# A fused retention and SwiGLU kernel: rows through GpSimd's queue, paired attention units, one PSUM rotation, half groups

## The chip, the cores and the metric

One core of one Trainium2 chip. The metric is device time in microseconds (us) of one execution, smaller is better. Most executions of one kernel agree within 1%; where one is over 1.5% above the fastest of its kernel, it counts as slow and stays out of the ratios. Ratios are the mean time of one kernel's fast runs over the mean of the other's fast runs of the same rounds on the same chip, so they are not quite the ratio of the medians quoted beside them.

Engines: PE (matmul), PEld (its weight loads), DVE (vector), ACT (scalar), POOL (GpSimd), SP (only issues transfers here). "PE waits" is idle time of PE just before an instruction, put down to what released it.

## The reference, cut to what matters

```python
# q, k, v: (B=4, H=8, S=768, D=64) float32
for t in range(S):                                   # retention, decay gamma[h]
    state = gamma * state + k[:, :, t] (x) v[:, :, t]
    y[:, :, t] = scale * q[:, :, t] @ state
x = y as (3072 tokens, 512)
xn = x / sqrt(mean(x*x) + 1e-6) * rms_g
out = (silu(xn @ w_gate) * (xn @ w_val)) @ w_out     # d_ff = 1536
```

Both kernels cut the sequence into six chunks c0 to c5 of 128 positions and turn the retention of a chunk into matmuls: scores (k against q, masked), y = masked scores against v plus q against the running state, and kv, which is added to the state. A **unit** is one chunk of one batch entry with all eight heads. The FFN of a chunk works on 512 tokens (four units): 12 gate-value blocks of 4 + 4 matmuls of 512 columns, then 4 down projections of 12. A **slot** is one block or one down projection; the attention of the next chunk is put between the slots of the present one. Names in the code and the profile: qb and kb are rows of q and k in bf16, qT and kT their transposes; a_ps are scores and am masked scores; x is y scaled, rstd its normalising factor (made on POOL from a sum of squares), xn the normalised rows and xnT their transpose; sg and hT are a block's results, o_sb that of a down projection.

## The kernel before

```python
def load(c, b, after=None):                # rows in float32, by SP
    for name, src in (("q_f", q), ("k_f", k), ("v_f", v)):
        x = loads.tile([128, H, D], F32, name=name)
        nc.sync.dma_start(out=x, in_=...)
# ...
def cast(c, b):                            # POOL casts, SP transposes
    nc.gpsimd.tensor_copy(qb, q_f...)
    nc.gpsimd.tensor_copy(kb, k_f...)
    nc.gpsimd.tensor_tensor(out=vp, in0=v_f, in1=vdec..., op=ALU.mult)
    if c > 1:
        for n in "qk":
            nc.sync.dma_start_transpose(out=t, in_=d[n + "b"])
# ...
def piece_y(c, b):                         # y, state, kv; x; squares; rstd on POOL
# ...
def piece_n(c, b):
    nc.vector.scalar_tensor_tensor(out=xn, in0=x, scalar=d["rstd"], in1=g_bc, ...)
    nc.sync.dma_start_transpose(out=cur[c, "xnT"][...], in_=xn)      # c > 1
# ...
PLAN = dict(cast=(0, 1, 2, 3), t=..., a=(4, 6, 8, 10), y=(6, 8, 10, 12),
            n=(8, 10, 12, 13), x=(8, 10, 12, 14))     # slot of each piece, by unit
# ...
def gv(n):
    g_ps = fps.tile([128, GT], F32, name="g_ps", tag="ff")   # one PSUM bank each
    v_ps = fps.tile([128, GT], F32, name="v_ps", tag="ff")
# ...
def down(b, n0=0, n1=NFF):                 # own bank for each
    o_t[b] = fps.tile([128, DM], F32, name="o_ps", tag="ff")
    # ... matmuls
    nc.scalar.copy(o_sb, o_ps)
    nc.sync.dma_start(out=out_v[c, b], in_=o_sb)
# ... in the loop over slots:
            if c == 0 and i == 16:         # chunk 2's rows, after the w_out weights
                nc.sync.dma_start(out=g_bc, ...)
                for b in range(B):
                    load(2, b, after=landed["wo", 2])
            if 0 < c < NCH - 2 and i in (5, 7, 9, 11):
                load(c + 2, (i - 5) // 2)
```

In chunks 2 to 5 the q and k transposes of the next chunk are thus requested in slots 0 to 3, the xn transposes in slots 8 to 13, both from SP. Chunks 0 and 1 are transposed on PE.

## Time and profile before

250.92 us (250.68 to 251.89); the profiled execution has a span of 248.7 us.

| stage (first gate matmul to the next) | us | PE busy |
|---|---|---|
| head, to the first gate matmul | 24.4 | 14.1 |
| c0 | 41.1 | 38.8 |
| c1 | 39.1 | 35.7 |
| c2, c3 | 36.8 each | 35.7 |
| c4 | 35.5 | 34.8 |
| c5 and tail | 35.1 | 31.1 |

PE is nearly full after the head. SP issues 63 row loads in the background, and PE waits for one transpose only, for 2.3 us in c1. The lines that show this stand in the prediction below.

### The profile page before, as it was taken

The numbers are of one execution on the slowest core, as the hardware profiler recorded it, in microseconds if no ns is written. First come the engines' busy times: TensorE is split into PE (matmuls) and PEld (weight loads), VectorE is DVE, ScalarE is ACT, GpSimd is POOL, SyncE is SP. The second block draws the span as 40 slices with busy tenths as digits, with TensorE's granted clock in tenths as the row PEclk, the third lists the DMA queues.
The fourth block names the chain that finished last, engine by engine and source line by source line (L and its number), as shares of the span: only waits on it lengthen the run. The fifth ranks groups of instructions, "written<-read, shape, count | busy, mean of one in ns | idle before, by whom it ended". The sixth has DMA issues, their size and how long they took to land.

```text
span 248.7 us, 4121 instructions
## 1 busy us (share of the span) xinstructions
PE 225.9 (91%) x1495; PEld 114.4 (46%) x1521; DVE 128.1 (51%) x215; ACT 87.4 (35%) x170; POOL 95.2 (38%) x177
## 2 busy tenths in 40 slices
PE   1776999979996989999989999989999999999993
PEld 0553445545433545445544445544444444444443
DVE  4796337676234895036894046894047781134300
ACT  6365334531431242232342322433232422332221
POOL 8978144953850236910246910246900211000000
PEclk9997999999999999999999999999999999999999
DMA  9999999898997699955999356999453114200022
GB/s 140 174 195 203 196 219 221 151 199 167 218 290 109 144 222 189 229 127 87 213 209 175 127 131 98 199 207 209 122 115 66 21 21 129 86 0 0 0 87 86
DMA packets 108213, 35.94 MB, mean 145 GB/s; under 512 B 99040, under 2 KB 104928, under 8 KB 108192
## 3 DMA queue, kind: packets, MB, share of 16 engines
q1 hardware_dynamic: 95232, 29.24, 60.8%
q0 software_dynamic: 12288, 6.29, 19.0%
q8 instruction: 12, 0.20, 0.3%
q10 hardware_dynamic: 672, 0.13, 0.3%
q14 instruction: 9, 0.07, 0.1%
HBM read 28.58 MB, written 6.29 MB: 140 GB/s over the span
## 4 chain that ended last, share of the span: by engine, by line
PE 77%; DVE 10%; DMA 5%; issue 3%; ACT 3%; POOL 0%; SPq 0%; DVEq 0%; ACTq 0%
PE o_ps L361 24%; PE v_ps L338 21%; PE g_ps L335 21%; DVE am L219 4%; PE a_ps L215 3%; PE y_ps L232 2%; DMA v_f<-in_v_dram 2%; DVE x L247 2%; DMA k_f<-in_k_dram 2%; PE kv_ps L244 1%; PE y_ps L237 1%; DMA kT<-kb 1%; DVE xn L283 1%; PE o_ps L351 1%; PE qk_ps L199 1%
## 5 line engine op out<-in xcount | busy, mean ns | idle before, releaser
L341 DVE TENSOR_TENSOR hT<-sg,v_ps 128x512 bf16<-128x512 bf16 x72 | 49.4, 687 | 89.6 <-PE v_ps L338 83.2
L338 PE MATMUL v_ps<-xnT,wv_b 128*128 128x512 bf16 x282 | 73.4, 379 | 0.5
L335 PE MATMUL g_ps<-xnT,wg_b 128*128 128x512 bf16 x276 | 72.9, 380 | 0.4
L340 ACT ACTIVATE sg<-g_ps 128x512 bf16<-128x512 f32 x72 | 42.8, 594 | 63.7 <-PE g_ps L335 62.2
L361 PE MATMUL o_ps<-wo_b,hT 128*128 128x512 bf16 x269 | 60.8, 379 | 1.2 <-DMA wo_b<-in_moe_w_out_dram 0.8
L338 PEld LDWEIGHTS <-wv_b 128*128 128x128 bf16 x288 | 28.2, 98 | 34.0
L335 PEld LDWEIGHTS <-wg_b 128*128 128x128 bf16 x288 | 26.6, 98 | 31.5 <-issue 0.9
L361 PEld LDWEIGHTS <-hT 128*128 128x128 bf16 x276 | 26.6, 98 | 30.9 <-issue 0.8
L272 POOL TENSOR_SCALAR ms<-ssq 128x1 f32<-128x1 f32 x24 | 4.5, 189 | 92.4 <-ACT xsq L251 92.3
L251 ACT ACTIVATE xsq<-x 128x512 f32<-128x512 f32 x24 | 15.1, 630 | 48.7 <-DVE x L247 48.6
L219 DVE TENSOR_TENSOR am<-a_ps,causal 128x512 bf16<-128x512 f32 x48 | 30.8, 682 | 2.4 <-PE a_ps L215 2.4
L366 ACT COPY o_sb<-o_ps 128x512 f32<-128x512 f32 x23 | 13.5, 585 | 36.8 <-PE o_ps L361 30.7
L180 POOL TENSOR_TENSOR vp<-v_f,vdec 128x512 bf16<-128x512 f32 x20 | 20.7, 1037 | 3.4 <-DMA v_f<-in_v_dram 3.4
L268 POOL CAST st_b<-st_f 64x256 bf16<-64x256 f32 x40 | 17.3, 432 | 1.3
L247 DVE TENSOR_TENSOR x<-y_ps,ydec 128x512 f32<-128x512 f32 x24 | 16.4, 685 | 1.4 <-PE y_ps L237 0.8
L232 PE MATMUL y_ps<-vp,am 128*128 128x64 bf16 x192 | 12.0, 200 | 5.4 <-DVE am L219 5.1
L178 POOL CAST qb<-q_f 128x512 bf16<-128x512 f32 x20 | 12.1, 606 | 8.7 <-DMA q_f<-in_q_dram 7.9
L283 DVE SCALAR_TENSOR_TENSOR xn<-x,rstd,g_bc 128x512 bf16<-128x512 f32 x16 | 12.5, 784 | 5.5 <-POOL rstd L275 5.5
L232 PEld LDWEIGHTS <-am 128*128 128x128 bf16 x192 | 9.2, 101 | 13.1 <-DVE am L219 9.7
L275 POOL TENSOR_TENSOR rstd<-ms,mhalf 128x1 f32<-128x1 f32 x24 | 13.2, 552 | 2.0
L179 POOL CAST kb<-k_f 128x512 bf16<-128x512 f32 x20 | 12.2, 609 | 2.6 <-DMA k_f<-in_k_dram 1.7
L259 DVE TENSOR_TENSOR st_f<-st_f,kv_ps 128x512 f32<-128x512 f32 x16 | 10.8, 676 | 0.0
(60 smaller groups left out, 125.5 us busy)
## 6 DMA issues: line engine op xcount, KB each, us to landing
out_dram<-o_sb SPq DMA_DIRECT2D x23, 256.0 KB, 2.2
q_f<-in_q_dram SPq DMA_DIRECT2D x21, 256.0 KB, 4.8
k_f<-in_k_dram SPq DMA_DIRECT2D x21, 256.0 KB, 5.0
v_f<-in_v_dram SPq DMA_DIRECT2D x21, 256.0 KB, 5.1
wg_b<-in_moe_w_gate_dram POOLq DMA_DIRECT2D x4, 384.0 KB, 9.6
wv_b<-in_moe_w_val_dram POOLq DMA_DIRECT2D x4, 384.0 KB, 10.7
wo_b<-in_moe_w_out_dram POOLq DMA_DIRECT2D x3, 512.0 KB, 8.3
v_f<-in_v_dram POOLq DMA_DIRECT2D x3, 256.0 KB, 6.2
```

The source lines that it names most:

```text
L180: nc.gpsimd.tensor_tensor(out=vp, in0=v_f, in1=vdec[:, c, :, None].to_broadcast([128, H, D]), op=ALU.mult)
L219: nc.vector.tensor_tensor(out=am[:, i], in0=a_ps[i], in1=causal[:, None, :].to_broadcast([128, NHP, 128]), op=ALU.mult)
L232: nc.tensor.matmul(y_ps[:, h, :], d["am"][:, i, hp, :], d["vp"][:, h, :], start=first, stop=last, skip_group_check=True)
L247: nc.vector.tensor_tensor(out=x, in0=y_ps, in1=ydec[:, c, :, None].to_broadcast([128, H, D]), op=ALU.mult)
L251: nc.scalar.activation(xsq, x.rearrange("p h d -> p (h d)"), AF.Square, accum_out=ssq)
L268: nc.gpsimd.tensor_copy(st_b[b][r, :, i * 64:i * 64 + 64], st_f[b][r, :, i * 64:i * 64 + 64])
L283: nc.vector.scalar_tensor_tensor(out=xn, in0=x, scalar=d["rstd"], in1=g_bc, op0=ALU.mult, op1=ALU.mult)
L335: nc.tensor.matmul(g_ps, wg_b[:, s, sl], xnT[:, s, :], start=s == 0, stop=s == KS - 1)
L338: nc.tensor.matmul(v_ps, wv_b[:, s, sl], xnT[:, s, :], start=s == 0, stop=s == KS - 1)
L340: nc.scalar.activation(sg, g_ps, AF.Silu)
L341: nc.vector.tensor_tensor(out=hT[:, n, :], in0=sg, in1=v_ps, op=ALU.mult)
L361: nc.tensor.matmul(o_ps, hT[:, n, b * C:(b + 1) * C], wo_b[:, n, :], start=n == 0, stop=n == NFF - 1)
```

## The change

Its intent: fewer casts (a transfer by GpSimd's queue can cast float32 to bf16), less work on DVE in chunk 0 (the decay goes into the mask), fewer changes of PE's row tiling (two units per row-tiled phase), shorter holes (FFN blocks begin when three of the four units are ready; chunk 1 in two half groups of 256 columns) and one rotation of four two-bank PSUM tiles for everything. The diff, cut to its core:

```diff
-    aps = tile_pool(name="aps", bufs=4, PSUM);  fps = tile_pool(name="fps", bufs=4, PSUM)
+    psum = tile_pool(name="psum", bufs=1, PSUM)
+    def banks(name, dtype=F32):               # tiles p0..p3 in turn, two banks each
+        i = turn[0] % 4
+        turn[0] += 1
+        return psum.tile([128, 2, 512 ...], dtype, name=name, tag=f"p{i}")
-    i = nc.sync.dma_start(out=x, in_=src[b]...)            # float32, then casts on POOL
+    def load(c, b, names="qkv"):
+        nc.gpsimd.dma_start(out=x (bf16 for q and k), in_=srcs[n][c, b])
+    def t_dma(c, b):
+        for n in "qk":
+            nc.sync.dma_start_transpose(out=t, in_=u[n])
+    nc.scalar.activation(mask0, marg, AF.Exp, scale=1.0, bias=lnscale)   # decay in c0's mask
+    def pair_pe(c, bs, nxt=()):               # scores of next units, state and y of two
+    def gv(c, n0, n1, t0, t1):
+        ps = banks("gv_ps")                   # bank 0 gate, bank 1 value
+        nc.scalar.activation(sg, ps[:, 0, :m], AF.Silu)
+        nc.vector.tensor_tensor(out=HT..., in0=sg, in1=ps[:, 1, :m], op=ALU.mult)
+    def down(c, b, n0=0, n1=NFF):
+            if b % 2 == 0:
+                O[c] = banks("o_ps")          # two down projections share a tile
+        ps = O[c, b][:, b % 2, :]
@@ head @@
+    gv(0, 0, 1, 0, 384)
+    rstd(0, [3])
+    load_w(4, 6)
+    norm(0, 3)
+    x_pe(0, 3)
@@ chunk 1: steps 0 to 15 are 6 double blocks + 2 down, twice @@
+        0: [..., L(load, 2, 0)],   1: [..., L(load, 2, 1)],
+        2: [..., L(load, 2, 2), L(t_dma, 2, 0), L(t_dma, 2, 1)],   3: [..., L(load, 2, 3)],
+        6: [..., L(t_dma, 2, 2), L(t_dma, 2, 3), L(load, 3, 0), L(begin, 2)],
@@ chunks 2 to 5, d = c + 1 @@
+                3: [L(pair_pe, d, (0, 1), ((d, 2), (d, 3))), ...],
+                6: [L(norm, d, 0), L(norm, d, 1), L(x_dma, d, 0), L(x_dma, d, 1)]
+                   + [L(state_cast, 0), L(state_cast, 1), L(t_dma, d + 1, 0), L(t_dma, d + 1, 1)] * state,
+                9: [L(pair_pe, d, (2, 3), ((d + 1, 0), (d + 1, 1)) if state else ())] ...
+                11: [L(norm, d, 2), L(norm, d, 3), L(x_dma, d, 2), L(x_dma, d, 3)] ...
+                12: [L(t_dma, d + 1, 2), L(t_dma, d + 1, 3)] * state,
```

## The prediction

> **What bounds the kernel now.** I read the share of each engine first, then a table of busy time by stage, then the timeline of the matmul engine, then the waits. The page:
>
> ```profile
> PE 225.9 (91%) x1495; PEld 114.4 (46%) x1521; DVE 128.1 (51%) x215; ACT 87.4 (35%) x170; POOL 95.2 (38%) x177
> PE   1776999979996989999989999989999999999993
> PEclk9997999999999999999999999999999999999999
> ```
>
> PE is full except in the first four slices, so the end is set by PE's list of work plus the holes in it. The stages begin where the first gate matmul of each FFN chunk begins in the timeline (24.38, 65.4, 104.5, 141.3, 178.2, 213.8); the table cut there (start:end and length, then busy us of each engine with instruction counts, clock, DMA share, GB/s):
>
> ```profile
> 0.00:24.38 24.38, 14.11 (x133) 9.44 (x135) 17.09 (x42) 14.04 (x30) 20.38 (x39) 0.93 1.38 178
> 24.38:65.59 41.21, 38.96 (x285) 20.30 (x289) 22.54 (x36) 15.22 (x27) 21.74 (x40) 1.00 1.10 194
> 65.59:104.70 39.11, 35.75 (x238) 17.62 (x240) 20.58 (x32) 12.05 (x24) 18.35 (x33) 1.00 1.04 201
> 104.70:141.29 36.59, 35.46 (x235) 17.54 (x239) 20.49 (x32) 12.05 (x24) 14.61 (x29) 1.00 0.88 161
> ```
>
> The first 24.4 us are a chain through DMA, DVE, ACT and PE; after it every chunk is PE work. How much of a chunk is needed comes from start-to-start times in PE's timeline:
>
> ```profile
> 119.90 1.03 PE L335 MATMUL g_ps<-xnT,wg_b 128*128 128x512 bf16 x4
> 120.76 0.81 PE L338 MATMUL v_ps<-xnT,wv_b 128*128 128x512 bf16 x3
> 121.62 0.40 PE L232 MATMUL y_ps<-vp,am 128*128 128x64 bf16 x8
> 121.86 0.39 PE L237 MATMUL y_ps<-st_b,qT 128*128 128x128 bf16 x4
> 122.08 0.39 PE L244 MATMUL kv_ps<-vp,kb 128*128 128x128 bf16 x4
> 122.40 0.40 PE L215 MATMUL a_ps<-qT,kT 64*128 64x128 bf16 x8
> 122.73 1.04 PE L335 MATMUL g_ps<-xnT,wg_b 128*128 128x512 bf16 x4
> ```
>
> Four N=512 matmuls take 0.86 us, 0.216 each. An FFN chunk has 96 + 48 of them, 31.1 us; six chunks 186.7. One unit of attention takes 0.24 (y) + 0.22 (state) + 0.32 (kv, and the change to 64 rows) + 0.33 (scores, and the change back) = 1.11 us. Four N=128 matmuls need 0.22, so each change of row tiling costs about 0.1 us. Transposes on PE, for chunks 0 and 1 alone, add 0.45 + 0.22 per unit. Needed and measured: c0 31.1 + 4 x 1.78 = 38.2 of 41.0; c1 31.1 + 4.4 = 35.6 of 39.1; c2 and c3 35.6 of 36.8 and 36.9; c4 (no kv) 34.7 of 35.6; c5 31.1 of 31.1. So **9.7 us are holes**. The waits name the largest ones:
>
> ```profile
> PE y_ps L232 <- DVE am L219: 5.1, 14, 0.5
> PE a_ps L215 <- DMA kT<-kb: 2.3, 1, 2.3
> ```
>
> The last unit of each chunk is scheduled with one FFN slot between scores and their use, while DVE is behind; and in c1 a transpose by DMA queued on SP behind late input. The last matmul begins at 244.6 and 3.8 us of eviction, store and end follow.
>
> **What the Trainium skill says.** "TensorE: Matmul & The Clock Gate", Back-to-back issue gap, gives N/2.4 + 2.5 ns for a warm matmul, 215.8 ns at N=512 and 109.2 at N=256; the trace agrees with the first (0.216 us). "TensorEngine Tiling (Array Packing)", Key Properties: "Mode switching requires drain"; the trace agrees, with the 0.1 us above. "PSUM — Partial Sum Buffer", PSUM bank collisions, wants two engines kept off one bank and quadrant; the trace shows the order kept: the half copies of qk_ps, one bank, ran ACT from 6.79 and DVE only from 7.41. "DMA: Bandwidth & Descriptors", SWDGE vs HWDGE, says that a cast in a DMA must come from GpSimd, which builds the descriptors; the trace shows GpSimd held 0.9 us by each such load.
>
> **The change, part by part.**
>
> *Rows via GpSimd.* It removes 40 casts (12.1 + 12.2 us) from POOL and adds 63 issues of about 0.9 us = 57 us; the state cast becomes one instruction instead of two (17.3 us becomes an estimated 12). POOL then has about 125 us over 245, no bound on average. On the wire it helps: in the slice 6.0 to 6.5 us, cast rows alone in flight,
>
> ```profile
> q0 software_dynamic: 616, 0.08, 245.3%
> ```
>
> 616 packets per half microsecond, so 0.85 us for a 1024-piece q or k; v takes 1.2 us by the same reading. Before, SP's rows moved 0.11 MB per half microsecond, 1.17 us each. A unit falls from 3.5 to 2.9 us. In steady chunks this was hidden anyway, but the late transposes of c1 (2.3 us) should go: issue comes earlier and nothing waits for a cast.
>
> *Head.* POOL's issue rate decides it:
>
> ```profile
> 4.87 0.90 POOL L78 DMA_DIRECT2D qb<-in_q_dram  x1
> 10.09 0.83 POOL L149 DMA_DIRECT2D wg_b<-in_moe_w_gate_dram  x1
> 12.36 0.57 POOL L275 TENSOR_TENSOR rstd<-ms,mhalf 128x1 f32<-128x1 f32 x1
> ```
>
> Issue starts at 0.9 us; twelve loads, the first 1.1, the others 0.88 pitch, and two iotas (0.35) end at 12.05. I take q at 4.7 and k at 5.7. Transposes, copies and scores: 7.2; mask 1024 wide (two of 0.6 pitch) 8.45. Unit 1's scores end at 9.6, y0 at 9.95, its squares at 10.8. But rstd of unit 0 must wait for POOL: 12.05 to 12.85. Then two weight issues (1.6), rstd 1 (0.8), two more (1.6), vp of unit 2 on POOL (1.05): 17.9. y, squares 19.1, rstd 19.95; DVE still has mask 3 until 21.25, norm 22.0, transposes and copies 22.85; y3 and kv of units 0 and 1: 23.4, warm-up, first gate matmul near **23.8** instead of 24.4. Against that, unit 3's normalisation and two kv stand between the first FFN pieces (0.3 + 0.45 us and narrow matmuls): block n=2 begins at 28.5, where before it began at 27.8. So "three batches on" gains almost nothing: what the missing y-scaling (0.69 us of DVE per unit) frees is lost to POOL's queue. I call the head +0.7 us.
>
> *Decay in the mask.* Four DVE x instructions (2.7 us) go, one exp over 1024 elements and one 1024-wide multiply come, during the wait for q. It is inside the head above.
>
> *Pairs.* Per pair: scores 16 x 0.027 = 0.43, state 0.4 in the same row tiling, y 0.48, kv 0.44, changes 0.2: 1.95 against 2.22; 10 pairs give about 2.5 us. The state matmuls have half the columns, but the y matmuls show 0.03 us each at 64 columns, so no more than that is to be had.
>
> *Order and PSUM.* Scores of the next pair are made one pair early (six FFN slots ahead), so y never waits for its mask. One rotation of four two-bank tiles: a gate-value block leaves its banks about 1 us after its last matmul, a mask pair 2.6 us after, and a tile comes round after four. Following a steady chunk slot by slot (1.73 us each; DVE 0.7 hT, 2.4 masks, 1.2 y, 1.2 kv, 1.4 norm) I find waits of 0.3 us in all. Holes of 1.2 + 1.3 + 0.9 in c2 to c4 become about 1.0.
>
> *Half groups.* Chunk 1 uses 192 N=256 matmuls: 192 x 0.1092 = 21.0 against 20.75 us, +0.2. It lets units 2 and 3 of chunk 1 move beside its first half.
>
> **Sum.** Block n=2 at 28.5; ten blocks 17.3, hole 0.5: 46.3. Down of c0 10.4, half of chunk 1's attention 3.3, hole 1.0: 61.0. Chunk 1: 21.0 + 10.4 + other half 3.2 + chunk 2's attention and chunk 3's first scores 4.4 + holes 1.5: 101.5. c2, c3: 31.1 + 3.5 + 0.4 = 35.0 each. c4 33.5, c5 31.1, end 3.85: span 240.0. The time before was 2.2 above its span (250.92, 248.7), so **242.2 us**; I put 242.0. The gain of 8.9 is mostly holes (9.7 to about 4.5), 2.5 from pairs, the rest from work that is shifted, less 0.7 in the head.
>
> **Rivals.** (a) *POOL's queue becomes the wait*: rows, weights, vp, rstd and state casts stand in one order, and an issue that waits for a buffer holds rstd behind it. For: the head chain above is POOL's, and ms waited 92 us for squares with the queue empty behind it; now loads stand there. Against: 12 issues x 0.9 + 4 vp x 1.04 + 3 + 2.5 = 20 us of 35 per chunk. If two stages lose 2.5 us each: 247. (b) *The single PSUM rotation stalls gate-value blocks* when DVE is behind, in c1 above all, where DVE has an estimated 21 us in eight slots of about 21 us: +3 to +5, 246. (c) *Weights come late*, since rows and rstd stand before them: before, 0.39 MB pieces landed 2 us apart, and I find each 2 to 5 us ahead of use; if not, +2, 244. (d) *The head does gain* because first rows land sooner or DVE is the true bound, which is now lighter: FFN at 21, total 239. (e) *All holes vanish*: 237.
>
> **Range and chances.** d and e go below, a to c above, each perhaps one in four, rarely together: 236.5 to 247.0. Faster by over 2% needs under 245.9: that fails if a or b is full size, so 0.80; same 0.17; slower 0.03, since over 10 us of new waits would be needed beside the gains.
>
> **What would show it.** Right: first gate matmul at 23 to 25 us, n=2 near 28.5; steady chunks 34.5 to 35.5 with PE waits for am gone; two changes of row tiling per pair of 0.1 us; c1 39 to 41 us; POOL near 125 us busy. Wrong: gate matmuls waiting for hT, masks or o_sb (b), rstd or vp late on POOL with xn behind it (a), waits for wg_b or wv_b (c).

## The result, and the profile after

The changed kernel takes **308.82 us** (305.24 to 310.06, 4 runs) against 251.4 (250.68 to 253.13, 4 runs) for the kernel before on the same chip: ratio 1.2183 (95% interval 1.2086 to 1.228). It is slower by 22%, where 4% faster was predicted. The profiled execution is the slowest of the four (1.6% above the fastest, so it counts as slow); its losses are tens of us and come back in the profiles of fast runs below (c1 takes 66.8 us in `own` and 67.0 in `norm`, c2 46.8 in `norm`).

The page of the changed kernel, shares and PE's slices:

```profile
PE 243.4 (79%) x1718; PEld 129.1 (42%) x1718; DVE 126.9 (41%) x203; ACT 85.4 (28%) x171; POOL 124.9 (41%) x163
PE   4656899979947399179991989990989999899994
PEclk9999799999989579859997899998799999999999
```

PE is idle for 65 us, in deep holes (3, 1, 1, 0) that lie in c1 to c3, and its granted clock falls in or after each. By stage (start:end and length; busy us of PE, PEld, DVE, ACT, POOL with counts; granted clock; DMA share; GB/s):

```profile
26.91:71.25 44.34, 38.80 (x253) 19.41 (x252) 17.43 (x28) 14.07 (x28) 26.06 (x35) 0.96 1.06 143
71.25:141.27 70.02, 48.06 (x449) 32.68 (x448) 31.53 (x42) 14.67 (x32) 42.45 (x50) 0.83 1.25 126
141.27:188.09 46.82, 37.69 (x258) 18.23 (x257) 20.16 (x28) 11.95 (x24) 18.76 (x24) 0.93 0.59 79
...
235.83:271.77 35.94, 34.00 (x225) 15.84 (x224) 15.39 (x22) 11.84 (x24) 1.76 (x4) 1.00 0.19 59
```

Against the prediction's steps: block n=2 begins at 36.85 instead of 28.5 (+8.35); from there to c1 34.4 instead of 32.5 (+1.9); c1 70.0 instead of 40.5 (+29.5); c2 46.8 and c3 47.7 instead of 35.0 (+11.8, +12.7); c4 35.9 instead of 33.5 (+2.4); c5 and tail 36.5 instead of 34.95 (+1.6). The sum is 68.3, which is 308.3 less 240.0. The stages that overshoot most are those whose q and k are transposed by transfer: c1, c2, c3 each prepare such a chunk; c4 has no further chunk to transpose for and overshoots by 2.4 us only.

The waits of the changed kernel (engine, line, what it waited for: us in total, times, longest):

```profile
PEld L194 <- DMA kT<-kb: 37.2, 10, 7.9
PE a_ps L194 <- DMA kT<-kb: 33.6, 9, 7.4
PE o_ps L356 <- ACT o_sb L360: 7.0, 11, 0.7
```

Before, the row for kT had 2.3 us once. The masks, for which y waited 5.1 us before, cost 0.7 now. PE's timeline of c2 shows one such stop and what follows it:

```profile
160.30 1.03 PE L338 MATMUL gv_ps<-xnT,wv_b 128*128 128x512 bf16 x4
167.89 0.61 PE L194 MATMUL a_ps<-qT,kT 64*128 64x128 bf16 x8 [6.57 <-DMA kT<-kb]
...
170.70 1.88 PE L338 MATMUL gv_ps<-xnT,wg_b 128*128 128x512 bf16 x4
```

Four matmuls of the same shape take 1.03 us before the stop and 1.88 after it: the clock is at about half. In c1 the scores wait 3.9, 6.6, 3.3 and 4.8 us, and down projections of 12 matmuls take up to 5.3 us instead of 2.75. SP's timeline of the same stretch says why kT was late:

```profile
158.77 2.50 SPq L272 DMA_TRANSPOSE xnT<-xn  x2
161.36 1.22 SPq L167 DMA_TRANSPOSE qT<-qb  x1
162.67 1.31 SPq L167 DMA_TRANSPOSE kT<-kb  x1
164.07 1.23 SPq L167 DMA_TRANSPOSE qT<-qb  x1
165.39 1.22 SPq L167 DMA_TRANSPOSE kT<-kb  x1
```

Every DMA transpose holds SP for about 1.25 us. SP is idle until the normalised rows (xn) exist at 158.77, then issues two xn transposes, then q, k, q, k: 7.8 us in single file. From the place of the request (slot 6) to the use (slot 9) PE has three slots, 5.2 us, and 2.8 of them are gone when xn is ready. The first kT is issued at 162.67 and lands 5.2 us later, which ends PE's wait. The rows themselves were there long before: POOL had issued their loads by 137.1. In the head, PE's timeline:

```profile
31.28 0.40 PE L261 MATMUL x_ps<-ident,xn 128*128 128x128 bf16 x4 [1.83 <-DVE xn L248]
32.62 1.44 PE L338 MATMUL gv_ps<-xnT,wg_b 128*128 128x384 bf16 x4 [0.95 <-ACT st_f L275]
```

DVE's order has the eviction of the first block (30.00) ahead of unit 3's normalisation (30.47), and the 384-column matmuls run at half clock. What was right: POOL is busy 124.9 us (predicted 125), and no matmul waits for a weight in c1 and later. The pairs came out dearer than predicted: in c2 scores, state and y take 1.57 us of PE from the end of one block to the start of the next, and kv 0.55, so 2.1 together (predicted 1.95; two single units took 2.22 before).

### The profile page after: what moved, and what is told of

The parts are those of the page before. It is cut to its first block, busy times and chain, and to the rows that moved or that the text cites. A ratio compares the mean times of both kernels' runs of the same rounds, so it can differ in the third digit from the quotient of the medians.

```text
span 308.3 us, 4342 instructions
## 1 busy us (share of the span) xinstructions
PE 243.4 (79%) x1718; PEld 129.1 (42%) x1718; DVE 126.9 (41%) x203; ACT 85.4 (28%) x171; POOL 124.9 (41%) x163
## 4 chain that ended last, share of the span: by engine, by line
PE 48%; DMA 16%; POOL 10%; ACT 7%; issue 7%; DVE 6%; SPq 5%; POOLq 0%; ACTq 0%; DVEq 0%
PE gv_ps L338 25%; PE o_ps L356 16%; DMA kT<-kb 9%; SPq L167 5%; DMA kb<-in_k_dram 4%; DMA v_f<-in_v_dram 3%; POOL qb L73 3%; DVE hT L343 2%; ACT sg L342 2%; ACT o_sb L360 2%; ACT xsq L231 2%; POOL vp L159 2%; POOL kb L73 2%; DVE x L318 2%; PE a_ps L194 2%
## 5 line engine op out<-in xcount | busy, mean ns | idle before, releaser
L343 DVE TENSOR_TENSOR hT<-sg,gv_ps 128x512 bf16<-128x512 bf16 (+2 forms) x73 | 49.5, 679 | 120.1 <-ACT sg L342 120.1
L338 PE MATMUL gv_ps<-xnT,wg_b 128*128 128x512 bf16 (+3 forms) x344 | 78.1, 358 | 2.6 <-DVE x L318 1.4
L338 PE MATMUL gv_ps<-xnT,wv_b 128*128 128x512 bf16 (+3 forms) x344 | 76.2, 351 | 0.0
L342 ACT ACTIVATE sg<-gv_ps 128x512 bf16<-128x512 f32 (+2 forms) x73 | 42.9, 588 | 114.0 <-PE gv_ps L338 114.0
L338 PEld LDWEIGHTS <-wv_b 128*128 128x128 bf16 x344 | 34.4, 101 | 30.9 <-issue 2.5
L194 PE MATMUL a_ps<-qT,kT 64*128 64x128 bf16 x192 | 11.1, 259 | 37.4 <-DMA kT<-kb 33.6
L206 DVE TENSOR_TENSOR am<-a_ps,causal 128x1024 bf16<-128x1024 f32 x20 | 23.6, 1218 | 27.1 <-PE a_ps L194 27.0
L73 POOL DMA_DIRECT2D qb<-in_q_dram x24 | 22.5, 938 | 0.9 <-POOLq L597 0.8
L70 POOL DMA_DIRECT2D v_f<-in_v_dram x24 | 22.1, 926 | 0.4 <-issue 0.3
L73 POOL DMA_DIRECT2D kb<-in_k_dram x24 | 21.8, 906 | 0.0
L282 POOL CAST st_b<-st_f 128x512 bf16<-128x512 f32 x20 | 14.4, 743 | 10.7 <-DVE st_f L278 6.3
L248 DVE SCALAR_TENSOR_TENSOR xn<-x,rstd,g_bc 128x512 bf16<-128x512 f32 x20 | 16.3, 855 | 1.2 <-POOL rstd L240 1.2
L278 DVE TENSOR_TENSOR st_f<-st_f,kv_ps 128x512 f32<-128x512 f32 x16 | 10.3, 681 | 0.1
```

The costliest lines, as they stand in the source:

```text
L70: nc.gpsimd.dma_start(out=x, in_=srcs[n][c, b])
L73: nc.gpsimd.dma_start(out=x.rearrange("p (h d) -> p h d", h=H), in_=srcs[n][c, b])
L194: nc.tensor.matmul(a_ps[:, i, hp * 128:(hp + 1) * 128], u["kT"][r, hp, :], u["qT"][r, hp, :], start=True, stop=True)
L206: nc.vector.tensor_tensor(out=am.rearrange("p i a t -> p (i a) t"), in0=src, in1=m, op=ALU.mult)
L338: nc.tensor.matmul(ps[:, i, o:o + w], wt[:, s, n * 128:(n + 1) * 128], XT[c][:, s, t0:t1], start=s == 0, stop=s == KS - 1)
L342: nc.scalar.activation(sg[:, :m], ps[:, 0, :m], AF.Silu)
```

## The experiments

Theory: three orders are at fault, not the operations. (1) q and k transposes stand in SP's single file behind xn transposes and stores (about 33 us of waits, and half clock behind them). (2) Two banks of one tile wait as one. (3) In the head the last unit's normalisation stands behind the first block's evictions. Rivals: the row loads by GpSimd slow the transposes themselves; the leads are too short in any order; the rows through GpSimd are dearer in themselves. Four batches ran, each on one chip with its own runs of the kernel before: `own`, `early`, `norm`, `rows` (median of before 250.5); `all2`, `rows2`, `b13`, `norows` (251.7); `twoq`, `rows3`, `best` (250.4); `order`, `twoq2`, `best2` (251.2).

### own: each down projection from chunk 1 on has its own tile

```diff
-            if b % 2 == 0:
+            if b % 2 == 0 or c > 0:
                 O[c] = banks("o_ps")
 # down_last: likewise a tile for each of its two halves
```

> From chunk 1 on each down projection gets a PSUM tile of its own instead of sharing a two-bank tile with its neighbour. If the eviction of one bank holds the matmuls into the other bank of the same tile (11 waits of 0.67 us for o_sb in the changed kernel), those 7.0 us go and the span falls by 7 to 9 us, to about 300. If these waits are only the visible end of PE being late for another reason, they reappear elsewhere and the time moves by less than 2 us.

299.06 us (296.24 to 299.5), ratio 1.1894. The waits of a down projection for o_sb fall from 7.0 us to this row:

```profile
PE o_ps L356 <- ACT o_sb L360: 1.3, 2, 0.7
```

So the copy of bank 0 did hold the matmuls to bank 1: the dependency is kept per tile. The median gain is 9.8 us, more than the 5.7 of this row; in the two profiles 2.9 us of the rest lie in the head (n=2 at 33.93), where the clock was granted earlier in this run with nothing changed there.

### early: chunk 2's and 3's rows earlier, q and k transposes ahead of xn transposes and stores

```diff
+    load(2, 0); load(2, 1)          # beside c0's down projections, not in c1's steps 0 and 1
+    t_dma(2, 0); t_dma(2, 1); load(2, 2); load(2, 3)
-        2: [..., L(load, 2, 2), L(t_dma, 2, 0), L(t_dma, 2, 1)],
+        0: [..., L(t_dma, 2, 2), L(t_dma, 2, 3)],    # chunk 3 moved up in the same way
-                6: [..., L(t_dma, d + 1, 0), L(t_dma, d + 1, 1)]
+                4: [..., L(t_dma, d + 1, 0), L(t_dma, d + 1, 1)]
```

> Rows of chunks 2 and 3 are loaded earlier and the q and k transposes by DMA are issued ahead of the xn transposes and the stores in SP's order. Theory 1 (too little lead in SP's single file): waits of scores for kT fall from 33.6 us to under 5, the half-clock stretches behind them go (granted clock 0.93 to 0.98 or more), c1 falls from 70 to about 42 us, c2 and c3 from 47 to about 37; time about 260. Theory 2 (row loads from GpSimd slow the transposes on the wire whatever the order): landing stays at 5 us median and waits of 15 us or more remain; time above 280.

275.41 us (275.12 to 275.8), ratio 1.098: 33 us less. PE waits for no DMA-made kT any more, and chunks 2 and 3 take 38.0 us each, at full clock. The row of c2 in the table by stage:

```profile
125.58:163.57 37.99, 35.86 (x257) 17.24 (x256) 20.08 (x28) 11.95 (x24) 23.30 (x29) 1.00 1.11 114
```

A transpose still takes a median of 5.8 us to land. The waits went as theory 1 expected, but not the whole time (275 against some 260): c1 still takes 50.1 us, not 42. The edit has its own price: the loads of chunk 2 now stand on POOL ahead of an rstd in c0, and PE waits for that:

```profile
69.55 0.40 PE L261 MATMUL x_ps<-ident,xn 128*128 128x128 bf16 x4 [2.99 <-DVE xn L248]
```

### norm: unit 3's normalisation ahead of the first gate-value block

```diff
-    gv(0, 0, 1, 0, 384)
     rstd(0, [3])
     load_w(4, 6)
     norm(0, 3)
+    gv(0, 0, 1, 0, 384)
     x_pe(0, 3)
```

> In the head the normalisation of unit 3 stands ahead of the first FFN block's evictions in the order of ACT, POOL and DVE; nothing else changes. If DVE's order made PE idle between the first two FFN pieces, the transposes of unit 3 start near 28.5 us instead of 31.3 and block n=2 near 33.5 instead of 36.85; time 2 to 4 us less. If the clock or the weights are what holds the head, under 1 us.

303.38 us (301.29 to 304.69), ratio 1.2086: some 3 to 5 us less. Block n=2 begins at 33.37. The unit's transposes come at 29.24 instead of 31.28. Part of it is the clock: in this run the narrow matmuls were at full clock from 30.73 on, and `own`, without this edit, had that too and began n=2 at 33.93. So the order is worth 0.6 us at equal clock; whether the shorter stop is what lets the clock rise in time is likely (both runs with the edit, one of six without) but not shown.

### rows: the kernel before, with its rows of chunks 1 to 5 through GpSimd's queue

```diff
-        q_f ... nc.sync.dma_start(out=x (float32), ...)
+        qb  ... nc.gpsimd.dma_start(out=x (bf16), ...)       # same places in the schedule
-        nc.gpsimd.tensor_copy(qb, q_f); nc.gpsimd.tensor_copy(kb, k_f)
 # qb and kb get 10 buffers instead of 6
```

> The kernel before with one part of the change alone: rows of chunks 1 to 5 by GpSimd's queue with the cast in the transfer, no casts on GpSimd; order of everything else as before. If the change of queue is harmless by itself, 248 to 252 us, kT waits of about 2 us or less. If row loads on that queue delay the transposes or rstd by themselves, kT waits of 10 us or more and a time above 258.

261.34 us (259.02 to 263.54), ratio 1.0387. More than half of the 11 us is one stop, from the timeline of PE:

```profile
71.08 0.61 PE L306 MATMUL xt_ps<-ident,xn 128*128 128x128 bf16 x4 [6.50 <-DVE xn L296]
```

In POOL's timeline twelve issues (58.81 to 69.5, 0.9 us each) stand ahead of the rstd at 69.56. This is the prediction's rival (a), in the kernel before. The time fell in the expected slow range, but not by its sign: scores wait only 2.9 us for kT.

### all2: own, early and norm together

Two of chunk 2's loads moved behind the rstd that `early` held up; otherwise the three edits above.

> The three repairs together (own tiles for down projections, transposes early, normalisation of unit 3 first), with two of the four early row loads moved behind rstd in GpSimd's order. If the three losses are separate, 308.8 - 33.4 - 9.7 - 5.4 = 260.3, and about 3 us less for rstd no longer held: 257. If they overlap, 262 or more.

258.94 us (258.64 to 260.63), ratio 1.0297, span 256.9 at full clock. The single gains (9.8 + 33.4 + 5.4 = 48.6) are near the 49.9 us found, so the three losses hardly overlap. That holds to a few us only: 2.9 of `own`'s 9.8 are not its edit's, and the 3 us that `early` lost to rstd are back here. 17 us over the prediction are left. By stage in its timeline: n=2 at 33.28 (4.8 over), then to c1 34.1 (1.6 over), c1 47.7 (7.2 over), c2 and c3 36.3 and 36.4 (1.3 and 1.4 over), c4 34.3 (0.8), end 34.9. In c1 PE stops nine times, 6.9 us together; the longest:

```profile
85.33 2.76 PE L356 MATMUL o_ps<-wo_b,hT 128*128 128x512 bf16 x12 [2.56 <-DVE st_f L278]
```

A down projection waits for the PSUM tile that DVE has yet to empty: rival (b). Even mended, the change is 3% slower than the kernel before: its steady chunks gain only 0.4 us each and c4 1.2, while c1 loses 8.6 and the first gate matmul comes 2.3 later.

### rows2: rows, with chunk 2's loads behind the rstd of chunk 1's last unit

```diff
             if c == 0 and i == 16:
-                for b in range(B): load(2, b, after=landed["wo", 2])
             for f in a_slots[i]: f()                # has the rstd
+            if c == 0 and i == 16:
+                for b in range(B): load(2, b, after=landed["wo", 2])
```

> Kernel before with rows by GpSimd's queue, and the twelve loads of chunk 2 issued behind rstd of chunk 1's last unit instead of ahead of it. If the 10.8 us that the queue cost came from rstd waiting behind twelve issues (the transposes of xn waited 6.5 us), the wait goes and the time is 250 to 254. If issue on that queue costs by itself, it stays at 258 or more.

259.81 us (258.82 to 262.1), ratio 1.0327: missed. The wait for xn is gone, and another of the same size is there, because the rows and so their transposes now come too late:

```profile
83.81 0.61 PE L224 MATMUL a_ps<-qT,kT 64*128 64x128 bf16 x8 [7.30 <-DMA kT<-kb]
```

### b13: the kernel before, last y and normalisation of a chunk one slot later

```diff
-    y=(6, 8, 10, 12), n=(8, 10, 12, 13), x=(8, 10, 12, 14)
+    y=(6, 8, 10, 13), n=(8, 10, 12, 14), x=(8, 10, 12, 15)
```

> Kernel before with the last unit's y one slot later, behind the first down projection, so that its mask is ready. The waits for am of 0.87 us in c1 to c4 each and their delay of the eviction go: 247 to 249. If xn then comes too late for the next chunk, 251 or more.

247.79 us (247.02 to 249.37), ratio 0.9848 (0.9776 to 0.9921): clearly under both kernels, though a gain of 2% is not established. The holes that the prediction found at the last unit are gone from c1 on, while a wait of 1.4 us for the last xn transpose appears at the start of c2.

### norows: the changed kernel without row loads of chunks 4 and 5

Wrong (chunk 3's rows used again, relative error 0.83): it takes the row loads out of c2 and c3.

```diff
+        if c > 3:
+            U[c, b] = {n: U[3, b][n] for n in names}
+            return
```

> Wrong on purpose: the changed kernel without the row loads of chunks 4 and 5 (they use chunk 3's rows again). In c2 and c3 no row load is on the wire when the q and k transposes go. If row loads slow them, landing there falls from 3.5 to 5.2 us to about 2.4 and the wait of scores for kT from 7 to about 5 us in each of the two chunks; if only SP's single file counts, both waits stay at 6.5 to 7.8 us.

305.17 us in the one run (state unknown). The transposes of c2 and c3 now land in 2.5 us (median), against 4.2 and 5.2 (k and q) in the same stretch of the changed kernel. So row loads do slow them. But PE still waits for most of the time:

```profile
162.72 0.61 PE L197 MATMUL a_ps<-qT,kT 64*128 64x128 bf16 x8 [3.93 <-DMA kT<-kb]
165.38 0.61 PE L197 MATMUL a_ps<-qT,kT 64*128 64x128 bf16 x8 [2.04 <-DMA kT<-kb]
```

5.97 us against 6.57 + 0.38 for the same pair in c2, and 6.2 against 7.8 in c3. This lies between the two expectations: the row loads on the wire account for 1.0 and 1.6 us. The rest is the late issue and the 2.5 us that a transpose takes to land even without them.

### twoq, twoq2: the k transposes through ACT's queue

```diff
-            nc.sync.dma_start_transpose(out=t, in_=u[n])
+            (nc.sync if n == "q" else nc.scalar).dma_start_transpose(out=t, in_=u[n])
```

> The changed kernel, with the k transposes of chunks 2 to 5 issued by ACT's queue instead of SP's; the loads, the order and the leads are as they were. Theory (SP's single file): two 1.25 us issues fewer stand between a pair's request and its last kT, and k no longer waits for q; the waits for kT in chunks 2 and 3 (6.6 to 7.4 us each) fall to 2 to 4 us and their sum from 33.6 to under 20; the time falls from 308 to 288 to 298. Rival (the transposes land late whatever their queue, for want of DMA engines or because they are requested too late): the waits stay within 1.5 us of what they were and the time is 304 or more, with up to 3 us of ACT time added.

329.64 us; the timed runs 323.03, 327.16 and 332.13, and the profiled one 828.64, with all matmuls at about a quarter of the speed from the first on (four of 512 columns start 3.3 us apart instead of 0.86), so its profile is no use. The theory is missed. The rival's "304 or more" holds as a number, but its 3 us of ACT time do not explain some 20 us more than the changed kernel takes. The kernel was run again for a profile:

> The kernel of `twoq` once more, for a profile of an ordinary execution: the profiled one there ran its matmuls at a quarter of the speed from the first on (829 us against 323 to 332 in the timed ones) and tells nothing. Expected time 323 to 332. Theory now: ACT's queue holds each k transpose until rows or other transfers have landed, and silu behind it, as the stores did in `best`; the profile shows idle time of ACT of some us ahead of or behind the transposes, and PE waiting for sg or gv_ps. Rival: transposes from two queues land far later (over 6 us for half of them), and PE waits for kT.

328.48 us (327.32 and 329.64). What SP waited for:

```profile
SPq L272 <- DMA kT<-kb: 52.7, 5, 16.5
SPq L167 <- DMA kT<-kb: 27.2, 7, 7.6
```

SP's xn and q transposes wait 79.9 us in all for ACT's k transposes to land. The Trainium skill, "DMA: Bandwidth & Descriptors", section "Silent corruption: two transposing streams in flight at once", says that a stream's first transpose must wait until the other's have landed; this trace shows such waits and their price. ACT was held up as well, once for 10.3 us ahead of a silu. So a second queue is no second lane for transposes. The run does not tell the theories apart; `order` does.

### rows3: rows, with chunk 2's loads spread over four slots

```diff
+            if c == 0 and i in (13, 15, 17, 18):
+                load(2, (13, 15, 17, 18).index(i), after=landed["wo", 2])
```

> The kernel before with its rows of chunks 1 to 5 through GpSimd's queue, chunk 2's twelve loads now spread: three each after the pieces of four slots around the last two normalisations of chunk 1, so that no more than three stand ahead of an rstd. Theory (in `rows` the rstd waited behind the loads, in `rows2` the loads and so the transposes came too late; both are only order): neither wait over 3 us is left, 251 to 255. Rival (twelve loads at 0.9 us don't fit on GpSimd there, or row loads by this queue cost more in themselves): a wait of 4 us or more on kT or xn stays in some place, 257 to 261.

254.74 us (253.02 to 255.86), ratio 1.0153, within the theory's range. The longest stop after the head is

```profile
81.04 0.40 PE L224 MATMUL a_ps<-qT,kT 64*128 64x128 bf16 x8 [2.75 <-DMA kT<-kb]
```

So some 60% of what `rows` lost (10.8 us of the medians, now 4.3) was order on POOL. The remaining 1.5% stays unexplained in detail; no gain from the saved casts shows in the time.

### best: b13, stores through ACT's queue, chunk 2's rows two slots earlier

```diff
-            nc.sync.dma_start(out=out_v[c, b], in_=o_sb)
+            nc.scalar.dma_start(out=out_v[c, b], in_=o_sb)
-            if c == 0 and i == 16:
+            if c == 0 and i == 14:
```

> The kernel before with the last normalisation of a chunk one slot later (as in `b13`), its stores of output through ACT's queue instead of SP's, and chunk 2's rows requested two slots earlier. If SP's single file is what holds the 1.8 us wait for kT in chunk 1 and the 1.4 us wait for xnT at the start of chunk 2 in `b13`, both go: 243.5 to 246.5. If those transposes are late for another reason, or ACT's issues hold up silu: 247 to 250.

254.8 us (254.07 to 255.74), ratio 1.0162: missed. The waits for kT and xnT are gone, but silu and copies now stand behind stores in ACT's order, and three of their waits end only when row loads or a transpose have landed (4.0 and 3.6 us of silu, 3.3 of a copy):

```profile
75.66 1.86 PE L335 MATMUL g_ps<-xnT,wg_b 128*128 128x512 bf16 x4 [3.24 <-ACT sg L340]
```

### order: one line of the changed kernel moved

```diff
-                6: [L(norm, d, 0), L(norm, d, 1), L(x_dma, d, 0), L(x_dma, d, 1)]
-                   + [L(state_cast, 0), L(state_cast, 1), L(t_dma, d + 1, 0), L(t_dma, d + 1, 1)] * state,
+                6: [L(t_dma, d + 1, 0), L(t_dma, d + 1, 1)] * state
+                   + [L(norm, d, 0), L(norm, d, 1), L(x_dma, d, 0), L(x_dma, d, 1)]
+                   + [L(state_cast, 0), L(state_cast, 1)] * state,
```

> The changed kernel with one line moved: in chunks 2 and 3 the q and k transposes of the next chunk's first pair are put ahead of the two xn transposes of the same slot, instead of behind them. The slot, the loads and the queue stay, chunk 1 stays. Theory (SP's single file: the q and k transposes could go long before, but stand behind xn transposes that wait for the normalisation): SP issues them as soon as it is free, before the slot is reached; the waits for kT of 6.6 and 7.4 us in chunks 2 and 3 are gone, with the half clock behind them: each of the two chunks falls from 47.3 to 38 to 41 us, the total from 308 to 289 to 296. Rival (three slots are too short a lead for transposes in any order, or they land late for want of DMA engines): only the two xn issues are saved, 2.5 us a chunk, 302 to 306.

**288.17 us** (287.2 to 289.04), ratio 1.1469: 20.6 us from a move within one slot, just under the theory's 289 to 296. SP's timeline:

```profile
140.69 1.21 SPq L167 DMA_TRANSPOSE qT<-qb  x1
142.00 1.22 SPq L167 DMA_TRANSPOSE kT<-kb  x1
143.32 2.21 SPq L167 DMA_TRANSPOSE qT<-qb  x1
145.62 1.22 SPq L167 DMA_TRANSPOSE kT<-kb  x1
154.48 13.63 SPq L272 DMA_TRANSPOSE xnT<-xn  x4
```

The same transposes are now all issued 7.6 us before the xn transposes, though the program still names slot 6: SP runs ahead of PE until something in its file has to wait. c2 and c3 fall to 38.1 and 38.0 us, the length they have in `early`; the row of c2:

```profile
136.90:175.00 38.10, 35.70 (x254) 17.25 (x257) 20.07 (x28) 11.94 (x24) 18.77 (x24) 1.00 0.88 104
```

Between the two profiles c2 and c3 give 18.6 us. Over the whole run the transposes land no faster (median of kT 5.8 us against 4.9). The first kT is issued at 142.00 and used at 156.98, so even the longest landing, 9.0 us, would be in time. So both rivals, slow landing and too few slots in any order, are refuted for these two chunks; what helps is not three slots but the 15 us that SP's running ahead gives. c1 is untouched and still has 16 us of waits for kT; `early` removes them, but it moves rows, order and lead together.

### best2: b13, chunk 2's pieces one slot later

```diff
+    PLAN2 = dict(PLAN, a=(5, 7, 9, 11), y=(7, 9, 11, 13), n=(9, 11, 13, 13), x=(9, 11, 13, 14))
```

> `b13`, with chunk 2's scores, y and normalisations (which run beside chunk 1's FFN) one slot later, and the last one's normalisation in the slot of its y. The 1.8 us wait for kT should go, since the transposes land in time for the later slot, and most of the 1.4 us wait for xnT, since the last xn transpose now stands ahead of a store: 244.5 to 246.5. If the wait only moves with the slot, 247 to 248.

247.28 us (246.6 to 249.5), ratio 0.9868 (0.9813 to 0.9924). The wait for kT is gone, and the one for xnT grew:

```profile
104.08 1.02 PE L337 MATMUL g_ps<-xnT,wg_b 128*128 128x512 bf16 x4 [2.09 <-DMA xnT<-xn]
```

The wait moved with the slot: no better than `b13` within the intervals. By shifting a plan, both are 1.3 to 1.5% under the kernel before, which is less than the 2% that counts as faster here, and some 60 us under the changed kernel.

## Why the prediction was wrong, point by point

- **"Scores of the next pair are made one pair early ..., so y never waits for its mask."** This step failed most. The mask waits did go (5.1 to 0.7 us). But scores that come early need kT early, and the step followed DVE and PSUM slot by slot, never SP. SP had 48 transposes of 1.25 us before too; new was that xn transposes stood ahead of q and k, with three slots to go. Cost: 33 us in waits and half clock, of which `order` takes back 20.6 by the order alone, most of it in c2 and c3. The other part lies in c1.
- **"The late transposes of c1 (2.3 us) should go: issue comes earlier and nothing waits for a cast."** The opposite happened: 18.8 us of kT waits in c1 (`order` still has 16.3). No run separates their causes, but SP's timeline of the changed kernel shows three. The first stop (3.9 us) is late rows: the kT that it needs was issued at 82.26 and took 8.1 us to land beside row loads. At the second (6.6 and 0.3) the transposes stood behind a store at 95.79 and were requested one slot before their use. At the third (3.3 and 4.8) they stood behind xn transposes, as in c2. Why the rows were late: POOL stood idle from 53.8 to 65.0 for a sum of squares, with the loads of chunk 2 behind it in program order, and issued them from 70.09 to 81.8. Rival (a) named this queue, but for rstd behind loads; here loads stood behind rstd. `rows`, `rows2` and `rows3` show both sides of that trade.
- **"A gate-value block leaves its banks about 1 us after its last matmul", "waits of 0.3 us in all".** Assumed bank by bank; the tile of two banks waits as one: 11 waits on o_sb, 7.0 us (`own` has 1.3 left), up to 9.8 us in all.
- **"First gate matmul near 23.8", "block n=2 begins at 28.5".** 26.91 and 36.85. Missing were the eviction ahead of the normalisation in DVE's order and the half clock of the first blocks; `norm` brings n=2 to 33.37. That leaves 4.9 us, which no run explains. The chain was behind its working from early on: in the changed kernel the first scores end at 8.4 us instead of 7.2, rstd of the third unit at 21.5 instead of 19.95, its normalisation at 24.3 instead of 22.0.
- **Rival (b), "+3 to +5" in c1**, was sound and is what remains in `all2`: 6.9 us of stops in c1, put down mostly to DVE.
- **"The gain of 8.9 is mostly holes."** In the mended kernel the steady chunks gain 0.4 us each, not 1.8. Part of the 1.3 us that c2 lacks is in the sum itself: it counts 3.5 for two pairs of 1.95, which are 3.9. A pair took 2.1, and two waits for DVE's x took 0.7 us where 0.4 of holes were allowed. Some 0.3 us stay open.
- **The chance of 0.03 for slower** rested on "over 10 us of new waits would be needed beside the gains". Nothing in the working checked the engine that issues the transfers, and what it left out cost 33 us.
- **Right**: POOL at 124.9 us (125), half groups at 0.109 us a matmul (0.875 us for eight in c1 of `all2`), no weight late. Near: pairs at 2.1 us (1.95), c4 at 34.3 in `all2` (33.5).

What stays open: how much of `norm`'s gain is order and how much the clock; the last 4 us of `rows3`; how c1's waits for kT divide between late rows, order and lead; and why the steps of the head came later than worked out.

## What to carry to other kernels

Treat every queue that issues transfers as an engine with a program order: list what stands ahead of each request, what that waits for, and what one issue costs; a request that could go early must not stand behind one that waits for computed data. When a piece of work is moved earlier, move all its inputs' requests earlier in the same step, in each queue they pass. And count release of buffers by the unit in which the program tracks them: two banks in one tile are one buffer.

## What the Trainium skill lacked or had wrong

- Page "DMA: Bandwidth & Descriptors": its transposes have a bandwidth, but for this chip and this size no cost for the queue that issues them. Here one of 128 x 512 bf16 holds SP for 1.2 to 1.3 us, against 0.3 to 0.6 for a store or load that waits for nothing; six in a row took 7.8 us, longer than the three slots (5.2 us) that they had.
- The same page asks for turns between two transposing streams; what they cost is not there. Here one queue waited 79.9 us in 325.5 for the other's transposes, and the kernel became 20 us slower, not faster.
- The same page gives no figure for how far row loads from GpSimd slow transposes beside them. Median landing of q and k transposes in c2 and c3 was 4.2 to 5.2 us with such loads in flight and 2.5 without (`norows`).
- No page has that a tile of two PSUM banks is released as one by the program's dependencies: 11 waits, 7.0 us.
- Page "TensorE: Matmul & The Clock Gate", section "Seeing it yourself", tells of the clock stuck at a quarter for over 50 us; one execution here (`twoq`) ran at about a quarter for all its 827 us, while the recorded granted clock said 1.0.
